# Two hand-written order lists of a fused attention and feed-forward kernel, written out anew

## The chip, the cores and the metric

The kernel runs on 1 core of one Trainium2 chip. The time is device microseconds (us). Before the change it is 468.69 us, the median of 3 runs (467.51 to 470.2). The profiled execution took 468.16 us.

## The reference

```python
def sm_attn(qq, kk, vv):
    s = scale * np.matmul(qq, kk.transpose(0, 1, 3, 2))
    s = s - np.max(s, axis=-1, keepdims=True)
    a = np.exp(s)
    a = a / (np.sum(a, axis=-1, keepdims=True) + 1e-09)
    return np.matmul(a, vv)
p_packed = sm_attn(p, k, v)                    # q, k, v: (8, 8, 576, 64), p: (8, 8, 32, 64)
out = sm_attn(q, p_packed, p_packed)
x = out.transpose(0, 2, 1, 3).reshape(4608, 512)
h = np.maximum(np.maximum(x @ w1, x @ w2), x @ w3)   # (512, 768) each
return h @ w_out                                     # (768, 512)
```

All data are float32. There are 8 batches (B) of 8 heads; a batch has 576 query rows.

## The kernel before, in words

The kernel works batch by batch. For each batch it computes the scores of the 32 packed queries with the keys (stage S), their softmax (A, Z), turns that round (X, by a write to DRAM and four reads back), multiplies it with the values (V), turns the result (K), computes the scores of the real queries (Q) and their softmax (B). The packed values are multiplied with the three weight matrices once for each of six column blocks j (stage P, `project`), and the result is multiplied with the attention weights (stage N, `layer_in`); halves and differences of the maxima (H) go through the output matrix (stage O, `layer_out`), and F adds up and stores. From batch 2 on, N is a product scheme with fewer multiplications (`layer_fast`), which needs sums of operands: T (`blend`) makes those of the attention weights, and `nine`, in P, those of the weights.

Nothing chooses the order at run time. Two strings, START (batches 0 and 1 and the conversion of the weights) and LOOP (one steady batch, run for batches 2 to 7), are lists of words, and `run` takes one word after the other. A word names a stage, the batch offset, the block and, by a last letter, an engine: v is VectorE (DVE), a is ScalarE (ACT), g is GpSimd (POOL). Each stage is a Python generator; each word carries it on to its next `yield`. So the words of N04 in LOOP are 19 steps of batch b, block 4, and `P10` is a step of the next batch, block 0. Each engine, and the DMA queue of SyncE (SP), gets its instructions in the order of the list, and works them off in that order. Where a word has the same stage and step in two lists, it issues the same instructions, but for the engine.

Small letters are loads on the SP queue: k keys, v values (two transfers each, L157 and L158), q queries, w weights at the start, m a block of the converted weights (768 KB, read back from DRAM, L171). `m03` to `m05` are blocks 3 to 5 of this batch, `m12`, `m10`, `m11` those of the next. The third word of X issues the write to DRAM (`xk<-x`, L315) and the four reads (`xt<-xk`, L319), which wait for that write.

Buffers are shared by tag. Tag "w" has six: they hold the m blocks, the scaled weights `pt` of `nine`, the sums `u` of `layer_fast` and the attention weights `e`. A tile that is asked for gets a buffer whose last tile is done, mostly the one done longest, so the order of the list also sets what each load waits for. In the list of before, `m05` gets the buffer of `u` of N00, which is free after the last join of N00 (L573 on DVE).

In `layer_fast`, three copies move sums out of PSUM (steps 7, 10 and 14, L118 on ACT, L120 on another engine):

```python
copy(u[:, 1], ps)            # step 7
join(u[:, 1], three, u[:, 1], ALU.max)
copy(u[:, 2], one)           # step 10, before product(one, (4, ...)), step 15
join(u[:, 0], two, u[:, 0], ALU.max)
copy(u[:, 3], ps)            # step 14
```

Of the kernel before, what the change touches and what calls it, by code (L numbers as in the profile page):

```python
# [47 lines left out]
B011v C10 C12 B010v N00 A10 N00 N00 A11 w20 w21 B001g B001 A10 C12 B000g A11 B011 Z10 E000a C10 A10v N00 A11a V101  # L48
C12 w22 C12 B001a q10 q11 B011v E000 C40 w52 B011g w51 Z11 C40 P01 E000 C41 V101 B001v P01 C42 k20 K1 C41 N00 C40
C40 E001a C42 N00 C41 w50 P01 C42 N01 k21 N01 C21 C20 N01 C20 C21 E010v E001 N01 C41 C42 w32 E010 P04 P04 C22 C20  # L50
K1v N01 C20 E001 w30 E011v E010 C22 N01 w31 P04 C52 Q1 N04 C21 C22 E011 H00g B11 N04 B10 B11 C52 w64 w60 C21 C22 N04
w65 C52 B10 C51 P02 E040a P02 E040 B11g B10g E011 C50 N04 N04 P02 E041a E040 N04 C51 B11 C50 C51 C50 v20 E041 N02 S2
N02 C51 B11 E041 N02 B10 C52 B11a B11 N02 C50 A20 H00a A21 B10 P05 P11 E020a v21 A20 A21 N02 B11g B10v C30 N02 P05
E020 C31 C32 C30 B10 X2 E021v w62 P05 H01g C32 N05 E021 N05 N05 B10g N05 C30 C30 E020 C31 E050a w63 C64 B11 E021 C32
P11 N05 C31 C64 B10 E050 B11a E050 N05 C32 P11 B10a B10v P12 C65 C31 E051a P12 C65 B11v X2 E051 Z21 P03 N11 N11
E110a N11 w61 N11 P03 E110 E111a H01g N11 N11 P03 N03 E030a P15 E110 H00v C62 D2g C65 H01v C61 P12 P15 P10 E051 H01v
H04g N03 C64 N03 H01a C65 N03 H02v E111 E030 Z20 N03 C62 C64 E031a N12 H04a E111 X2 P15 C60 N03 E030 N12 E031 W2v
H05a N12 C60 D5v W2v C60 W2v V201 H01g P10 P14 D5 H02a N12 E120a P10 C61 N12 N12 E121a E031 W2a C61 D1v H04v C60
E120 V201 E120 N15 H02v C63 N10 C61 N10 C62 P14 W0v N10 E121 P14 C63 C62 N14 C63 W0v C63 E100a E150a E140a E121 N14
E100 W1v N14 W2v N14 W1g E140 W2a E100 N10 N14 E140 W1g E101a W0v q21 H05v W1a E141a N10 W2v P13 K2 W1v E141 N15 q20  # L60
E101 W0a N15 N15 W1a W2g W0v W1v E151a W1g N10 H12v E150 P00 D3g E101 O0 W0a P13 F0a D3 E150 K2a H11a H03a N14 N15
W2a P13 H05v N13 k30 E130a H10v H05v D2 O0 H03v W1a N13 W0v Q2 H12a F0a E151 H05a H10a N13 O0 N13 H03v E141 E130 W1g
B20 B20 E130 B20v O0 P00 H14v W0g E131a N15 N13 N13 D0v H03g D4v O0 P20 B21 P21 O0 E151 H14a B21 F0a W2g E131 W0a
E131 H03a H12g H05v H03v H11g H10v P20a F0a H14g D0 B20 P20 F0 F0 O0 B20 P20 P20 B20a H15a O0 D1 F0 P20 O1 P20 B20
B21v B21 O1 F1a O1 H15v H15v O1 B20v H11g H13a F1a B21 B21a O0 P21a W0g H11g F1a F0 B21 H13v O0 H13v H15g B21v F0
P20a O0 F0 k31 F1v H13g B21 P21 H11a O0 B20 F0 P20v H11v H15a O1 P22 H13a F1 H15v H13g O0 F0 O1 O0 O1 O1 F0 F0 P22v
O1 P22 O1 O1 B20a B21a F1 T2g P22 F0 P21 F0 B21v P20a F1 T2g T2g F1 P20v F1 F1 O1 P22 F1 B20v D4 T2a F1 F1 T2g P22g
P21 P21g P22g F1 T2a P22a T2g P21g P21a P22g P21g O1 F1 O1 F1
"""


LOOP = """
S1 A11 N00 N00 N00a N00 N00a N00 N00a m03 N00 N00 N00a N00 A11 N00 A10 A10 N00 N00a N00 N00 N00 N00 m04 N01 N01
N01a m05 N01 N00 X1 N01a N01 N01a N01 H00g X1 N01 N01a H00a N01 N01 N01 H00g Z11 N01a N01 v10 N01 N01 N01 P03
N01 P03a P03 H01g H01g P03 P03 P03 P04 P04a P03 P04 P03g P05 P03g v11 N02 P04 N02 X1 N02a P04 N02 N02a P05a N02
N02a N02 q11 N02 P05 P05 N02a N02 N02 P03a N02 N02a k20 N02 P04a N02 H01g N02 N02 N03 N03 N03a N03 N03a P05 H01g
N03 P03g P04g N02 Z10 N03a N03 P04a N03 N03a N03 P04g q10 N03 N03 H02g P05a N03v N03 N03 N03 H01a N04 H02a N03
N04 N04a N04 N04a N04 H02v N03 H01v V101 V101 N04a H03a N04 N04 N04a N04 m12 K1 N04 N04 N04a K1v N04 N04 N04 Q1
N05 N04 N05 N04 P05g P05a N05a N05 B10 H04v N05a N05 H03g m10 N05a B10 P05v N05 B11 N05 H04a N05a N05 N05 N05
N05a H03g k21 B11 N05 N05 B10g H04g N05 N05 B11g P10 B10 P10a B10 P10 P12 P10 P10 B10v P10 N05 O0 F0a P10 O0  # L80
H05a H03v m11 B11 F0a H03a O0 H05v H05g O0 F0a B10 P11 H05v H03v O0 H05a O0 B11 H05v P11a F0a B11a P12a B11 P12
B10v F0 B10 F0 O0 P11 O0 F0a B11g O0 B11 P12 P10a P11 T1g F0a B10a B11a F0a O0 P11 T1g F0a O0 F0 B11v F0 P12 T1v
P11a P10v P10v T1a B10v O0 T1v T1a F0a O0 F0a T1g P10g P12a P12g P11g P12a P12g P11a O0 F0 F0 P11g
"""


# [780 lines left out]
```

## Time and profile before

| | |
|---|---|
| median of 3 runs | 468.69 us |
| profiled execution | 468.16 us |
| its span, first to last instruction | 466.4 us |
| PE (TensorE matmul) busy | 447.6 us, 96% |
| DVE busy | 396.7 us, 85% |
| ACT busy | 279.3 us, 60% |
| POOL busy | 262.2 us, 56% |
| mean granted TensorE clock | 0.996 of full speed |

The span is some 1.8 us shorter than the execution's time. PE is busy nearly throughout, so the few microseconds in which it is not are what an order can win or lose. Batches 0 and 1 end at about 141 us; then each steady batch takes 53 to 58 us, and the last one 50.

### The profile page before, as it was taken

The numbers are of one execution on the slowest core, as the hardware profiler recorded it, in microseconds if no ns is written. First come the engines' busy times: TensorE is split into PE (matmuls) and PEld (weight loads), VectorE is DVE, ScalarE is ACT, GpSimd is POOL, SyncE is SP. The second block draws the span as 40 slices with busy tenths as digits, with TensorE's granted clock in tenths as the row PEclk, the third lists the DMA queues.
The fourth block names the chain that finished last, engine by engine and source line by source line (L and its number), as shares of the span: only waits on it lengthen the run. The fifth ranks groups of instructions, "written<-read, shape, count | busy, mean of one in ns | idle before, by whom it ended". The sixth has DMA issues, their size and how long they took to land.

```text
span 466.4 us, 11887 instructions
## 1 busy us (share of the span) xinstructions
PE 447.6 (96%) x4592; PEld 388.5 (83%) x4592; DVE 396.7 (85%) x868; ACT 279.3 (60%) x639; POOL 262.2 (56%) x250
## 2 busy tenths in 40 slices
PE   8999999999999989999899999997999989998997
PEld 3467878998998878979799888986989878897997
DVE  2888999999987979988898989986899888987870
ACT  2687957554535737567476657754576564665652
POOL 0577775556587833856446653656337574385622
PEclk9999999999999999999999999998999999999999
DMA  8999872065248782297624784186741775235002
GB/s 305 402 381 410 281 245 81 1 199 229 84 171 282 206 341 74 92 303 237 239 85 157 275 293 178 52 264 196 265 153 66 275 208 199 69 109 197 1 2 101
DMA packets 31160, 89.89 MB, mean 193 GB/s; under 512 B 3072, under 2 KB 16384, under 8 KB 31104
## 3 DMA queue, kind: packets, MB, share of 16 engines
q1 hardware_dynamic: 31104, 89.14, 54.9%
q8 instruction: 36, 0.59, 0.5%
q14 instruction: 20, 0.16, 0.1%
HBM read 71.43 MB, written 17.69 MB: 191 GB/s over the span
## 4 chain that ended last, share of the span: by engine, by line
PE 80%; DMA 10%; DVE 7%; issue 1%; ACT 0%; POOL 0%; SPq 0%; DVEq 0%; POOLq 0%
PE mo L713 29%; PE mi L644 9%; PE mi_b L567 8%; PE mi_a L567 7%; PE pw L526 5%; DMA w<-wk 5%; DMA q<-in_qt 5%; PE mi_f L567 5%; PE mi_d L567 4%; PE idle L131 3%; PE mi_c L567 3%; PE s L367 2%; PE s L253 2%; DVE r L658 1%; DVE u L573 1%
## 5 line engine op out<-in xcount | busy, mean ns | idle before, releaser
L678 POOL TENSOR_TENSOR r<-r 128x288 f32<-128x288 f32 (+1 forms) x43 | 42.2, 982 | 38.2 <-DVE r L573 28.9
L567 PE MATMUL mi_b<-a2h,pt 128*128 128x288 f32 x216 | 47.1, 304 | 0.0
L526 PE MATMUL pw<-w,pt 64*32 64x384 f32 x768 | 38.2, 491 | 8.3 <-DMA w<-wk 7.7
L118 ACT COPY u<-mi_b 128x288 f32<-128x288 f32 x36 | 14.4, 400 | 52.9 <-PE mi_b L567 52.9
L573 DVE TENSOR_TENSOR u<-mi_d,u 128x288 f32<-128x288 f32 x72 | 32.4, 451 | 13.0 <-ACT u L118 9.0
L713 PE MATMUL mo<-ych,xh 128*128 128x288 f32 x144 | 42.6, 296 | 0.3 <-DVE r L735 0.3
L713 PE MATMUL mo<-ych,xl 128*128 128x288 f32 x144 | 42.6, 296 | 0.0
L713 PE MATMUL mo<-ycl,xh 128*128 128x288 f32 x144 | 42.1, 292 | 0.0
L567 PEld LDWEIGHTS mi_b<-a2h,pt 128*128 128x128 f32 x216 | 34.7, 190 | 8.4 <-issue 5.3
L644 PE MATMUL mi<-a2h,ph 128*128 128x288 f32 x132 | 40.4, 306 | 0.8 <-DVE r L658 0.8
L644 PE MATMUL mi<-a2l,ph 128*128 128x288 f32 x132 | 38.9, 295 | 0.6 <-DVE a2l L123 0.6
L644 PE MATMUL mi<-a2h,pl 128*128 128x288 f32 x132 | 39.0, 295 | 0.0
L481 DVE SCALAR_TENSOR_TENSOR pt<-pw,pt 128x384 fp32r<-128x384 f32 (+1 forms) x48 | 34.5, 747 | 4.4 <-ACT pt L479 4.3
L485 DVE SCALAR_TENSOR_TENSOR pf<-pw,pf 128x128 f32<-128x128 f32 (+1 forms) x108 | 35.8, 332 | 2.5
L207 POOL TENSOR_TENSOR w<-w,wi 128x512 int32<-128x512 int32 x18 | 23.7, 1327 | 23.2 <-ACT wi L192 17.3
L567 PE MATMUL mi_b<-a2l,pt 128*128 128x288 f32 x108 | 32.1, 297 | 0.0
L123 POOL TENSOR_TENSOR ps<-pf,ps 128x384 fp32r<-128x384 f32 x30 | 30.3, 1017 | 2.5 <-ACT ps L118 2.0
L567 PE MATMUL mi_a<-a2h,pt 128*128 128x288 f32 x144 | 31.0, 297 | 0.0
L479 ACT ACTIVATE pt<-pw 128x384 fp32r<-128x384 f32 (+1 forms) x48 | 29.6, 658 | 2.2 <-DVE pf L507 1.9
L567 PE MATMUL mi_f<-a2h,pt 128*128 128x288 f32 x144 | 30.3, 299 | 0.0
L644 PEld LDWEIGHTS mi<-a2h,ph 128*128 128x128 f32 x132 | 24.8, 188 | 6.5 <-issue 2.3
L401 POOL TENSOR_TENSOR e<-e,m 128x576 f32<-128x576 f32 (+1 forms) x15 | 15.9, 1070 | 24.2 <-DVE m L399 24.1
(180 smaller groups left out, 1582.8 us busy)
## 6 DMA issues: line engine op xcount, KB each, us to landing
w<-wk SPq DMA_DIRECT2D x33, 768.0 KB, 5.5
kt<-in_kp SPq DMA_DIRECT2D x16, 640.0 KB, 6.9
wi<-in_wi SPq DMA_DIRECT2D x18, 512.0 KB, 8.1
v<-in_va SPq DMA_DIRECT2D x16, 512.0 KB, 7.5
q<-in_qt SPq DMA_DIRECT2D x14, 576.0 KB, 6.4
wk<-w SPq DMA_DIRECT2D x6, 768.0 KB, 5.2
xk<-x SPq DMA_DIRECT2D x6, 576.0 KB, 7.9
wi<-in_wo SPq DMA_DIRECT2D x6, 512.0 KB, 4.4
```

The lines of the kernel that those rows point to most:

```text
L123: on(default).tensor_tensor(out=lo, in0=src, in1=hi.bitcast(F32), op=ALU.subtract)
L207: nc.gpsimd.tensor_tensor(out=dst.bitcast(I32), in0=dst.bitcast(I32), in1=up, op=ALU.add)
L401: on("g").tensor_tensor(out=e3, in0=e3, in1=m.unsqueeze(2).to_broadcast([P, nt, NP]), op=ALU.subtract)
L479: nc.scalar.activation(out=t[:, 0, r], in_=y, func=AF.Copy, scale=2.0 ** -WS)
L481: nc.vector.scalar_tensor_tensor(out=t[:, 1, r], in0=y, scalar=2.0 ** -WS, in1=t[:, 0, r].bitcast(F32), op0=ALU.mult, op1=ALU.subtract,)
L485: mix = lambda out, a, c, op: nc.vector.scalar_tensor_tensor(out=out, in0=a, scalar=2.0 ** -WS, in1=c, op0=ALU.mult, op1=op,)
L526: nc.tensor.matmul(out=ps[r][NP * n:NP * n + NP, 0:NW * P], lhsT=pt_sb[b % 2][o, NP * n:NP * n + NP], rhs=w[o, n * NW * P:(n + 1) * NW * P ...
L567: nc.tensor.matmul(out=out, lhsT=x, rhs=y, start=(start and k == 0 and n == 0), stop=(stop and k == len(terms) - 1 and n == 2), skip_group ...
L573: join = lambda out, x, y, op: nc.vector.tensor_tensor(out=out, in0=x, in1=y, op=op)
L644: nc.tensor.matmul(out=sums[b, j, hf, x][:, 0:HS], lhsT=w[:, r, x * P:(x + 1) * P], rhs=a[:, c], start=(r == 0 and n == 0), stop=(r == R - ...
L678: less = lambda out, x, y: on("g").tensor_tensor(out=out, in0=x, in1=y, op=ALU.subtract)
L713: nc.tensor.matmul(out=ps[:, 0:HS], lhsT=w[:, x, m * P:(m + 1) * P], rhs=h[:, z], start=(not chain and p == 0 and i == 0), stop=(p == NQ - ...
```

## The change

Both lists hold the same words as before in another order (START from its eighth line on, 660 words; LOOP, 285 words), and some words name another engine. No instruction is added or removed. In LOOP, what changes on each queue is this:

- PE: P04 and P05 stand behind the first two products of N02 (before: ahead of them); V101 stands behind the 15th step of N04 (before: behind the 6th), K1 after the step that follows it; Q1 stands behind the first product of N05 (before: ahead of it); P11 stands behind the sixth O0 (before: behind the fourth). All else is in the same order.
- SP before: m03, m04, m05, v10, v11, X1 (write and reads), q11, k20, q10, m12, m10, k21, m11, stores. After: m03, m04, v10, m05, X1, v11, q10, q11, m10, m12, k20, k21, m11, stores.
- Buffers of tag "w", by the order of the list: `m05` gets that of `pt` of block 0, free after step 15 of N00 (PE); `m10` that of `m05`, free after P05; `m11` that of `pt` of block 5, free after step 15 of N05.
- Engines: copies 7, 10 and 14 of N00, 14 of N01 and 10 of N04 go from ACT to DVE, 14 of N03 from DVE to ACT; K1's copy goes from DVE to ACT; five splits (of H01, H04, P10, B11 and the first of T1) go from DVE to POOL, two (P04, P05) from POOL to DVE; some smaller copies change too.

```diff
 LOOP = """
-S1 A11 N00 N00 N00a N00 N00a N00 N00a m03 N00 N00 N00a N00 A11 N00 A10 A10 N00 N00a N00 N00 N00 N00 m04 N01 N01
-N01a m05 N01 N00 X1 N01a N01 N01a N01 H00g X1 N01 N01a H00a N01 N01 N01 H00g Z11 N01a N01 v10 N01 N01 N01 P03
-N01 P03a P03 H01g H01g P03 P03 P03 P04 P04a P03 P04 P03g P05 P03g v11 N02 P04 N02 X1 N02a P04 N02 N02a P05a N02
...
-N04 N04a N04 N04a N04 H02v N03 H01v V101 V101 N04a H03a N04 N04 N04a N04 m12 K1 N04 N04 N04a K1v N04 N04 N04 Q1
-N05 N04 N05 N04 P05g P05a N05a N05 B10 H04v N05a N05 H03g m10 N05a B10 P05v N05 B11 N05 H04a N05a N05 N05 N05
...
+m03 S1 N00 N00 A11 N00a N00 m04 N00a N00 A10 v10 A11 N00v A10 N00 N00 N00v N00 m05 N00 N00 N00v N00 N00 N00 N00
+N00 N01 N01 N01a N01 N01a N01 X1 H00g H00g X1 N01a H00g N01 N01 N01a N01 N01 N01 N01v N01 N01 N01 P03 N02 N02
+P03a P04 N01 N01 P03 X1 P03 P03 P03 N02a P03 P05 N02 P04v N02a P04 N02 P05a P04 v11 N02a H01g P05 N02 H01g P04
+N02 N02a P03g q10 H01g N02 P03g q11 N02 P05 H01g m10 P04a N02 N02a N02 N02 N02 N03 N03 N03a N03 N03a N03 N02
...
+N04 N04 N04a N04 N04a N04 N04a P04a P05a N03 N04 N04 N04v N04 N04 H03a P04g k20 H02v Z10 N04 N04a N04 V101 H03g
+N04 V101 N04 K1 N04 N05 N04 K1a k21 Q1 N05 N05a N05 N05a H04v N05 P05v N05a B10 N05 B11 B10 N05 N05a N05 N05
...
```

START's lines change in the same manner, from the first H00 on: the order of the words of batches 0 and 1, of the last loads (w61 now ahead of w64, X2 ahead of w62 and w63, v20 behind them) and of the stores of the converted weights (D0 to D5), and some engines.

## Rows read from the trace of the kernel before

**Rows 1.** The page: the span, and section 1 (busy time, share, instructions).
```profile
span 466.4 us, 11887 instructions
PE 447.6 (96%) x4592; PEld 388.5 (83%) x4592; DVE 396.7 (85%) x868; ACT 279.3 (60%) x639; POOL 262.2 (56%) x250
```

**Rows 2.** Busy time by stretch: its length, then each engine, PEclk, DMA.
```profile
80.00:100.00 20.00, 19.21 (x154) 18.15 (x153) 19.48 (x39) 12.37 (x24) 9.29 (x8) 1.00 0.24 80
...
140.80:195.30 54.50, 52.89 (x574) 46.99 (x581) 48.11 (x107) 34.14 (x83) 32.55 (x33) 1.00 0.60 205
195.30:250.40 55.10, 52.74 (x572) 46.87 (x576) 49.24 (x109) 33.97 (x83) 30.46 (x31) 1.00 0.58 197
250.40:303.60 53.20, 52.81 (x570) 46.94 (x570) 48.87 (x109) 34.08 (x83) 30.63 (x31) 1.00 0.59 204
303.60:361.10 57.50, 54.24 (x573) 48.35 (x576) 49.03 (x109) 34.08 (x83) 30.45 (x31) 0.97 0.56 189
361.10:416.00 54.90, 52.67 (x567) 46.94 (x567) 48.78 (x109) 33.96 (x83) 30.46 (x31) 1.00 0.52 173
```

**Rows 3.** Who PE waited for: us in total, times, longest.
```profile
PE pw L526 <- DMA w<-wk: 7.7, 4, 3.2
PE s L367 <- DMA q<-in_qt: 2.7, 3, 1.2
```

**Rows 4.** The chain that ended last, batch 3: start us, us, what.
```profile
195.29 1.13 PE s L253 x32
...
200.19 0.41 PE mi_a L567 x3
...
202.43 5.41 DMA w<-wk
...
216.20 8.66 DMA q<-in_qt
```

**Rows 5.** The same chain in batches 4 to 7.
```profile
250.42 1.13 PE s L253 x32
...
260.52 2.14 PE pw L526 x48
262.66 0.99 PE mi_b L567 x6
...
310.78 7.55 DMA w<-wk
...
319.25 1.74 PE mi_b L567 x6
...
368.26 6.53 DMA w<-wk
...
422.15 5.71 DMA w<-wk
```

**Rows 6.** The SP queue in batch 3: start us, us, what.
```profile
213.23 1.97 SPq L319 DMA_DIRECT2D xt<-xk  x4
```

**Rows 7.** Time to landing: the w issued at 198.0, the v at 205.1.
```profile
DMA to landing us min/median/max: 6.8/6.8/6.8
...
DMA to landing us min/median/max: 6.5/6.5/6.5
```

**Rows 8.** DVE, then weight loads of PE, after V101 in batch 3.
```profile
221.12 0.48 DVE L349 TENSOR_SCALAR pp<-av,r 128x64 f32<-128x64 f32 x2 [0.56 <-PE av L339]
...
221.75 0.14 PEld L354 LDWEIGHTS av<-ident,pp 128*128 128x128 f32 x1
```

**Rows 9.** DVE from 141 to 416 us by form: busy us, mean ns.
```profile
L123 DVE TENSOR_TENSOR a2l<-e,a2h 128x576 fp32r<-128x576 f32 x15 | 18.2, 1236 | 0.0
...
L266 DVE TENSOR_REDUCE mx<-s 128x1 f32<-128x576 f32 x10 | 7.5, 746 | 0.8 <-PE s L253 0.8
...
L123 DVE TENSOR_TENSOR ybl<-r,ybh 128x576 fp32r<-128x576 f32 x5 | 3.8, 751 | 0.0
...
L120 DVE COPY u<-mi_f 128x288 f32<-128x288 f32 x5 | 2.3, 456 | 1.0 <-PE mi_f L567 1.0
```

More of the change, by code (lines that the diff above doesn't have):

```diff
@@ L50 @@
 C40 E001a C42 N00 C41 w50 P01 C42 N01 k21 N01 C21 C20 N01 C20 C21 E010v E001 N01 C41 C42 w32 E010 P04 P04 C22 C20
[L51 to L68, printed above, removed]
+K1v N01 C20 E001 w30 E011v E010 C22 N01 w31 P04 C52 Q1 N04 C21 C22 E011 E011 H01a N04 H00g C21 N04 B10 H00a B10 C22
@@ new lines @@
+E040a B11 E040 P02 B11 C51 H00v C51 v21 N04 C51 C52 B10g B11v w61 P02 C50 E041a N04 N04 C50 C50 C52 C50 P02 B11 C32
+w64 C32 B10 B11 S2 E040 w60 N02 w65 E041 A20 A21 C30 A20 N02 B11a C51 B10 N02 C32 H01v H01g C52 E020a A21 E020 P05
+P11 X2 C31 N02 P05 P05 B10a E021a C30 E020 C32 N02 B10 H01g N05 C30 C31 X2 B11 N05 C61 E041 C64 B10g C31 B11v E021
+P12 C60 N05 C31 E050a P11 C30 B10 E050 B11 N05 N02 C61 P11 N05 B10a E051a C64 X2 w62 B11a C65 E021 B10g N05 E051
+B11v C65 P03 w63 H02v P03 N11 N11 E051 C65 P12 E050 H01a N11 v20 P03 C64 N11 E110a H01v P15 E110 N03 C60 N11 E111a
@@ new lines @@
+P12 C65 C60 N11 C61 E030a C63 E111 N03 P15 N03 N12 C63 H02a C64 N03 Z20 C62 E111 N12 N03 V201 C61 E030 E110 Z21 P10
+E030 C60 W2v N03 E031a H04v C62 D5v W0v W0g P15 E031 W2v N12 W2g H11a E120a N12 H02v W0v C62 C63 W2a E031 E120 P10
+N12 N12 H05a E121a V201 P10 P14 E120 C62 C63 W1g N15 W2v P14 H03a E121 E150a P14 N10 E121 N15 W0a W1g E150 E100a
+H04a K2 P13 N14 W1v H12v W0v H05g E140a N15 N14 N10 N14 W2a D4g D4 N10 W0a N10 N15 N10 N14 E150 E100 E140 D5 H04v
+W1a E101a N14 H03v q20 E100 E151a K2v N10 W2v q21 H05g E141a W1v W2g N14 E140 O0 E141 O0 W0g E101 W1a P13 E101 W1v
@@ new lines @@
+E141 P13 W0g O0 O0 H14v N13 D2v H03v Q2 H05v F0a F0a H03v H05a O0 D0v D1v N13 H05v B21 F0a O0 H10g H12a H14a B20 k31
+F0a F0 H11g E130a B21 E130 H03a B20 H12g D1 F0 N15 W2a W0a W2g N13 W0v N13 E151 B21v W1g N13 N15 N13 B20v H03v H10a
+H14v E131a E130 E131 H10g B21 P21 P22 E151 B20 H11g P20 P21a B20 E131 O1 O1 O1 O1 P20a H15a B21 P20 H11v O0 W1a W1v
+B21a D0 B21 F1a F1a H15v H13a B21v H15g F1a P22a D3v B20a H15v O0 O0 O0 P21 P20 F1a O0 H13g O0 P20 P20 F0 B20 P20
+H15a O0 H13g B20g B21 F0 F0 F0 H13g F0 H13a D3 H11a B20 F0 P21 O0 F0 P00 F0 H15v O1 H13v H11v F0 O1 B20a k30 T2v F0
@@ L69 @@
+O1 T2g B21a P21 P20a P00 P21a B20g F1 T2g O1 F1 P20g P22 F1 D2 F1 B21v T2a O1 O1 F1 F1 P22 P22 F1 F1 P21g O1 P21g F1
+O1 F1 T2g O1 P21g P22g O1 P20a T2a T2g P22g F1 P22a F1 P22v P20v
 """
 LOOP = """
-S1 A11 N00 N00 N00a N00 N00a N00 N00a m03 N00 N00 N00a N00 A11 N00 A10 A10 N00 N00a N00 N00 N00 N00 m04 N01 N01
-N01a m05 N01 N00 X1 N01a N01 N01a N01 H00g X1 N01 N01a H00a N01 N01 N01 H00g Z11 N01a N01 v10 N01 N01 N01 P03
-N01 P03a P03 H01g H01g P03 P03 P03 P04 P04a P03 P04 P03g P05 P03g v11 N02 P04 N02 X1 N02a P04 N02 N02a P05a N02
@@ L76 @@
-N02a N02 q11 N02 P05 P05 N02a N02 N02 P03a N02 N02a k20 N02 P04a N02 H01g N02 N02 N03 N03 N03a N03 N03a P05 H01g
-N03 P03g P04g N02 Z10 N03a N03 P04a N03 N03a N03 P04g q10 N03 N03 H02g P05a N03v N03 N03 N03 H01a N04 H02a N03
-N04 N04a N04 N04a N04 H02v N03 H01v V101 V101 N04a H03a N04 N04 N04a N04 m12 K1 N04 N04 N04a K1v N04 N04 N04 Q1
-N05 N04 N05 N04 P05g P05a N05a N05 B10 H04v N05a N05 H03g m10 N05a B10 P05v N05 B11 N05 H04a N05a N05 N05 N05
-N05a H03g k21 B11 N05 N05 B10g H04g N05 N05 B11g P10 B10 P10a B10 P10 P12 P10 P10 B10v P10 N05 O0 F0a P10 O0
@@ L81 @@
-H05a H03v m11 B11 F0a H03a O0 H05v H05g O0 F0a B10 P11 H05v H03v O0 H05a O0 B11 H05v P11a F0a B11a P12a B11 P12
-B10v F0 B10 F0 O0 P11 O0 F0a B11g O0 B11 P12 P10a P11 T1g F0a B10a B11a F0a O0 P11 T1g F0a O0 F0 B11v F0 P12 T1v
-P11a P10v P10v T1a B10v O0 T1v T1a F0a O0 F0a T1g P10g P12a P12g P11g P12a P12g P11a O0 F0 F0 P11g
+m03 S1 N00 N00 A11 N00a N00 m04 N00a N00 A10 v10 A11 N00v A10 N00 N00 N00v N00 m05 N00 N00 N00v N00 N00 N00 N00
+N00 N01 N01 N01a N01 N01a N01 X1 H00g H00g X1 N01a H00g N01 N01 N01a N01 N01 N01 N01v N01 N01 N01 P03 N02 N02
@@ new lines @@
+P03a P04 N01 N01 P03 X1 P03 P03 P03 N02a P03 P05 N02 P04v N02a P04 N02 P05a P04 v11 N02a H01g P05 N02 H01g P04
+N02 N02a P03g q10 H01g N02 P03g q11 N02 P05 H01g m10 P04a N02 N02a N02 N02 N02 N03 N03 N03a N03 N03a N03 N02
+P03g N02 N03a N03 P04v H01a N03 N03a Z11 P05 P03g H02g N03 N03 N03 N03a N03 N03 H02a N03 P05a N03 m12 P05v H01g
+N04 N04 N04a N04 N04a N04 N04a P04a P05a N03 N04 N04 N04v N04 N04 H03a P04g k20 H02v Z10 N04 N04a N04 V101 H03g
+N04 V101 N04 K1 N04 N05 N04 K1a k21 Q1 N05 N05a N05 N05a H04v N05 P05v N05a B10 N05 B11 B10 N05 N05a N05 N05
@@ L84 @@
+H04g H04g H03g m11 N05 N05a N05 B10g B11 N05 N05 P10 P12 O0 N05 P10a N05 O0 O0 P10 P10 P10 P12a P10 P10 O0 B10
+B10 H05a F0a H05v O0 F0a H03v H05g B11g B11 O0 B10v P11 H05v B10 B11 F0a P10a H03a H03v F0a H05a H05v B11a B11
+B10v P10g B10 P12 F0 B11g F0 B11 O0 F0a O0 P12 O0 P10a B10a T1g T1v T1v F0a B10v P11a O0 F0a F0a P11 T1a F0 F0
+O0 P12 B11a B11g P11 T1g O0 F0a P11 O0 F0a P11a P12a T1a F0 T1g O0 P12g P12a F0 P11g P10v P12g P11g P11g
 """
```

## The prediction

> **What bounds the kernel now.** I read the page first: PE is busy for 447.6 of 466.4 us, more than any other engine [rows 1], and the work of no engine changes in amount, only in place. So the change can only win the time in which PE stands still, or add to it. The table of stretches then shows where that is. A steady batch holds 52.8 us of PE work (52.89, 52.74, 52.81 and 52.67 in the four batches at full clock), but the five batches from 140.8 to 416 take 54.5, 55.1, 53.2, 57.5 and 54.9 us, together 275.2 [rows 2]. 275.2 less 5 x 52.8 is 11.2 us. The list of PE's waits names the cause: 7.7 us in four waits of `pw` for a block of weights, 2.7 us in three waits of Q1 for queries, and nothing else in the steady batches comes to 1.5 us [rows 3].
>
> The chain of waits shows how each comes about. In batch 3, the third block (m05) is issued at 202.43, when its buffer comes free behind three DVE joins that follow the product at 200.19 to 200.60; it lands at 207.84 [rows 4]. In batch 4 the three `pw` groups run unhindered, so P05 is due at 260.52 + 2/3 x 2.14 = 261.95, which is 11.5 us after S1 [rows 5]. In batch 3 that is 206.8, so PE waited 1.05 us. In the same way batch 5 (S1 at 303.6) waited until 318.33 instead of 315.1, 3.2 us, and batch 6 until 374.79 instead of 372.6, 2.2 us [rows 2, 5]; 7.7 less these leaves 1.25 for the last batch. The last query block in batch 3 is issued at 216.20 and lands at 224.86 [rows 4]; it stood in the SP queue behind the reads of X1, which began at 213.23 [rows 6].
>
> Behind the longest stop the mean granted clock of the batch is 0.97 [rows 2]: the first `mi_b` group takes 1.74 us where another takes 0.99 [rows 5]. The engine had stood still for 3.2 us before; the shorter stops, of 1 to 2.2 us, have no such row. These matmuls ran at the lower of the two levels (1.2 GHz, against 2.4). The row shows 0.75 us lost on the first six; PE's busy time in the batch, 54.24, is 1.5 above the mean of the others, 52.8 [rows 2], and I take that as the loss. So loads cost 11.2 + 1.25 = 12.5 us in all: 7.7 + 2.7 + 1.5 = 11.9, and 0.6 in small change.
>
> **The change part by part.**
>
> *m05 and P05.* The issue moves from 202.43 to 200.6 or so, 1.8 us, since the new buffer is free with PE's step 15 and not with the last DVE join [rows 4]. But two transfers of v10 now stand ahead of it. Their price: the last of two such pairs was issued at 205.1 and took 6.5 us, so it landed at 211.6 [rows 7], 3.8 us after the block at 207.84 [rows 4]: 1.9 us a pair. So the block lands when it did. The use moves: the first two products of N02, 9 matmuls, are put ahead of P04, some 0.8 + 0.4 us without the 0.2 for the change from narrow matmuls that is paid anyway [rows 4, 5]. Each wait shrinks by 1.2: batch 3 from 1.05 to 0, batch 5 from 3.2 to 2.0, batch 6 from 2.2 to 1.0. The last batch has no v10, so its block lands earlier and it waits 0. Left: 3.0 us. Bounds: 0, if the issue 1.8 us earlier counts as well; 9.8, if the pair comes on top without that gain (first rival). A stop of 2.0 us is among those that left the clock alone, so the 1.5 us go.
>
> The Trainium skill, page "DMA: Bandwidth & Descriptors", section "Anatomy of one DMA", puts a transfer at 2.0 us plus its bytes at 436 GB/s, measured for transfers issued by GpSimd. By it m03, m04, v10 and m05, 2.95 MB, would land 8.8 us after the first issue, no wait were left, and the sum would be 457.2. The trace does not bear it out here: m04, issued at 198.0, took 6.8 us [rows 7], so 1.57 MB landed at 204.8, about 7.6 us after the first issue, where the rule gives 5.6.
>
> *Queries and Q1.* The write of X1 no longer has v11 in front of it, so it lands a pair earlier, 1.9 us, and the reads begin near 211.3 instead of 213.23 [rows 6]. v11 comes next, then both query blocks without a key block between them; the bytes ahead of the last one are about the same (a v pair for k20), so it lands near 223. Q1 was due about 1.2 us before 224.86, stands one six-matmul product (0.8) later, and moves up by the 1.05 that P05 no longer waits: some 223.5. Wait 0 instead of 2.7. Bounds: 0 and 2.7.
>
> *v11 behind the reads.* It is issued near 213 and, at 6.5 us [rows 7], lands near 219.5. V101 ends at 221.05 today and takes 1.4; its place is 2.0 us later and the batch 1.05 earlier: due at 220.6. Cost 0, and nothing less; if v11 is late by more than 1 us, a microsecond a batch, at most 5.
>
> *K1.* Today two products (0.8 us) lie between V101 and K1, which turns what DVE makes of V101. DVE is done with it at 221.60, 0.55 after V101, and K1's weights load at 221.75 [rows 8]. Now one product of 0.4 us lies between. PE then waits 0.7 - 0.4 = 0.3 us, in five batches 1.5. Bounds: 0 and 2. The copy behind K1 goes to ACT; K1 and a copy of 0.3 fit under the product of 0.8 that now precedes Q1, at a cost of 0 to 1.5 if ACT is late. I take 0.
>
> *m10, m12, m11, keys.* m10 and m12 are issued earlier and used as before; m11 waits for N05's step 15 instead of P10, and P11 stands two products of O0 (2.4 us) later. All gain room; k20 and k21 are due a batch half later. 0, with no gain either, as PE never waited for them [rows 3].
>
> *Engines.* By the mean durations of like rows, DVE loses about 0.9 us a batch of 49, ACT 3.3 of 34, and POOL gains 4.3 on 30.5 [rows 2]. None reaches 52.8. So 0; what it costs if DVE is late at one place is the second rival.
>
> *START.* From 40 us on DVE is as full as PE (19.48 and 19.21 of 20 us in the stretch shown [rows 2]). The new engines take some 3 us from DVE, and PE's words are in quite another order. PE idles under 1 us in each such stretch, so there is little to win: 0, from -2 to +2.5. The upper end: V201 stands three PE words of some 0.8 us earlier, and waits that long if its loads, whose order changed too, come as before.
>
> *Sum.* The profiled execution took 468.16 us (its span of 466.4 and 1.8 around it), 0.5 under the median of the runs. 468.16 - 12.5 + 3.0 (P05) + 1.5 (K1) = **460.2 us**.
>
> **Rivals.** *The v pair is paid in full (no change).* If blocks queue strictly and the queue was full anyway, m05 lands 1.9 us later than today. Then P05 waits 1.75, 3.9 and 2.9 us in batches 3, 5 and 6 and 0.6 in the two others with v10, 9.8 in all, and the clock still falls once: 468.16 - 12.5 + 9.8 + 1.5 + 1.5 = 468.5. For it: m04, m05 and the v transfers landed in the order of issue, about 3 and 1.9 us apart [rows 4, 7]. Against it: m05 was issued 5.2 us after m03, and the queue had little to move before it began.
>
> *DVE is late in N00 (slower).* Copies 7, 10 and 14 of N00 go to DVE, behind two reductions of 746 ns with a small step each [rows 9]. From S1's end, at 196.4, 1.8 for these, 0.46 for copy 7, 0.45 for a join and 0.46 for copy 10 [rows 9] make 199.6 to 199.7; step 15, which needs copy 10, starts at 200.19 [rows 4]. So 0.5 us is spare. If DVE comes to S1 later than that, PE waits for the excess, in all six batches: at 2 us 12 us, 472.2. It decides against the change from 8 / 6 = 1.3 us on. For it: the split of `a2l` on DVE takes 1236 ns on average where a like split of `ybl` takes 751 [rows 9], so DVE is held up near a batch's start, and POOL gets more to do. Against it: that split is one that leaves DVE for POOL, and DVE's sum falls.
>
> The Trainium skill, page "SBUF — State Buffer", section "SBUF: two separate sides", says that DVE and GpSimd share one port pair, held for a whole instruction, and that a DVE operation with two SBUF inputs takes part in this. By that rule the three copies, which read PSUM, are not held up at all, and this rival would be worth nothing; the row of the split agrees with it, for the copies no run shows it here.
>
> *The opening loses, or the loads are all covered.* With START at +2.5 and Q1 not wholly covered, some 465; with no wait left at P05 and K1, 455.7.
>
> **How the numbers follow.** Forecast, 457 to 464: 0.55. All covered, 455.7: 0.10. Opening loses, 465: 0.08. The pair paid in full, 468.5: 0.15. DVE late, 472: 0.12. I hold half a percent, 2.3 us about the median of 468.7, for what a measurement can tell from no change. Faster: 0.55 + 0.10 + 0.08 = 0.73; same: 0.15; slower: 0.12. The range reaches from 455.0 to 468.6 and leaves out the slower case and a little below; beside it, the likeliest case's own range is 457 to 464.
>
> **What would show it.** In PE's waits, `pw` for `wk` at about 3 us instead of 7.7, in two waits, and Q1 for `q` gone; a granted clock of 1.00 in every stretch; steady batches of 53 to 55 us. In the chain, m05 issued 5.3 us after S1 instead of 7.1. A gap of 0.3 us between V101 and K1, ended by DVE's `pp`. Wrong would be waits of `pw` that stay above 6 us, a gap in N00 that ends with a DVE copy, or a first 141 us that grew by more than 2.5.

## The result, and the profile after

The changed kernel took 463.46 us (median of 4 runs, 463.06 to 463.78), the kernel before beside it 469.44: a ratio of 0.9871, 95% interval 0.9826 to 0.9917. The profiled execution took 463.06 us against 468.16. A second series (12 runs, given below) put the same kernel at 465.23 and a ratio of 0.9941 (0.9910 to 0.9971). So the change makes the kernel faster by something between 0.6 and 1.3% (the two intervals reach from 0.3 to 1.7%); the forecast of 460.2 had the direction and lies below both. Ratios, here and below, leave out runs that lie more than 1.5% above the fastest of the same kernel.

The page: the span, and the engines' busy time.

```profile
span 461.3 us, 11953 instructions
PE 451.7 (98%) x4592; PEld 387.7 (84%) x4592; DVE 395.4 (86%) x885; ACT 262.1 (57%) x600; POOL 283.0 (61%) x272
```

The five steady batches by stretch (columns as in [rows 2]).

```profile
139.50:194.00 54.50, 54.00 (x567) 47.02 (x566) 50.22 (x112) 30.16 (x75) 34.03 (x33) 1.00 0.58 204
194.00:248.30 54.30, 53.79 (x574) 47.09 (x579) 49.25 (x111) 31.04 (x78) 34.59 (x35) 1.00 0.57 200
248.30:302.50 54.20, 53.70 (x572) 46.99 (x573) 49.25 (x111) 30.97 (x78) 34.52 (x35) 1.00 0.57 200
302.50:356.70 54.20, 53.69 (x567) 46.99 (x566) 49.25 (x111) 30.95 (x78) 34.49 (x35) 1.00 0.57 200
356.70:410.90 54.20, 53.71 (x567) 47.18 (x567) 49.26 (x111) 30.98 (x78) 34.54 (x35) 1.00 0.50 176
```

Before, a batch took whatever the loads allowed, 53.2 to 57.5 us [rows 2]. Now all five are alike, 54.2 to 54.5, at full clock, and 271.4 together instead of 275.2. But none is near the 52.8 that the forecast took for a batch without load waits. The list of PE's waits from 141 us on says why:

```profile
PE mi_a L567 <- ACT mi_b L118: 1.8, 6, 0.4
PE mi_d L567 <- DVE u L573: 1.3, 6, 0.2
```

Both load waits of [rows 3] are gone, 10.4 us. In their place stand two waits that occur once in every batch, and PE's busy time in a batch is some 0.9 us higher than before: a matmul that starts late is in part booked as a long one, as the chain shows. This is the chain in batch 3 (start, us, what), at N01, at N02 and at K1, in three pieces. In it `mi_a` to `mi_f` are the PSUM banks of a product, `u` holds the sums copied out of them, `r` the maxima of a block; `pt` and `pf` are the scaled weights that `nine` makes.

```profile
199.86 0.47 DVE u L573
200.33 0.02 issue
200.35 0.77 DVE r L573
...
201.20 0.41 ACT u L118
201.61 0.02 issue
201.63 0.39 ACT mi_b L118
202.02 0.04 issue
202.07 0.67 PE mi_a L567 x3
...
209.44 0.96 DVE pt L481
210.39 0.21 DVE pf L485
210.60 0.02 issue
210.62 0.43 DVE pf L485
...
211.29 0.46 DVE u L573
211.75 0.04 issue
211.79 0.66 PE mi_d L567 x3
```

```profile
222.26 0.59 PE mi_d L567 x3
222.85 0.03 issue
222.88 0.33 PE av L354
```

First piece: the first copy of N01 (`u`, ACT) starts only when DVE has finished N00's last join (`r`, to 201.12), because it writes into the buffer of N00's `u`. That is the buffer that `m05` had before the change. `m05` now has the one that comes free earlier, and the wait that it used to bear has passed to N01's copy, then to the second copy (`mi_b`), then to PE: three `mi_a` matmuls take 0.67 instead of 0.40. Together with the gap before it that is 0.54 us a batch. Second piece: DVE makes P04's scaled sums (`pt`, `pf`) ahead of N02's join `u`, and N02's last product waits; 0.6 us a batch by the steps of N02. Third: K1, foreseen.

`m05` itself, with its time to landing, and P05's place on PE (the 32 narrow matmuls are P04 and then P05, 16 each, so P05 starts near 207.5):

```profile
L171 SPq DMA_DIRECT2D w<-wk x1: 320/320/320, 199.5 to 199.5; - x1
...
DMA to landing us min/median/max: 7.5/7.5/7.5
```

```profile
206.84 1.52 PE L526 MATMUL pw<-w,pt 64*32 64x384 f32 x32
```

It is issued 5.5 us after S1 (194.0), lands 12.9 us after it, and is used 13.5 us after it.

### The profile page after: what moved, and what is told of

It is laid out like the page before. It is cut to its first block, busy times and chain, and to the rows that moved or that the text cites. A ratio compares the mean times of both kernels' runs of the same rounds, so it can differ in the third digit from the quotient of the medians.

```text
span 461.3 us, 11953 instructions
## 1 busy us (share of the span) xinstructions
PE 451.7 (98%) x4592; PEld 387.7 (84%) x4592; DVE 395.4 (86%) x885; ACT 262.1 (57%) x600; POOL 283.0 (61%) x272
## 3 DMA queue, kind: packets, MB, share of 16 engines
q1 hardware_dynamic: 31104, 89.14, 54.2%
## 4 chain that ended last, share of the span: by engine, by line
PE 84%; DVE 7%; DMA 3%; ACT 2%; issue 2%; SPq 1%; POOL 0%; DVEq 0%; ACTq 0%; POOLq 0%
PE mo L713 30%; PE mi L644 12%; PE mi_a L567 8%; PE mi_b L567 7%; PE mi_d L567 6%; PE pw L526 6%; PE mi_f L567 5%; PE idle L131 3%; PE mi_c L567 2%; PE s L253 2%; PE av L339 2%; PE s L367 2%; DMA xk<-x 2%; DMA xt<-xk 1%; DVE pt L481 1%
## 5 line engine op out<-in xcount | busy, mean ns | idle before, releaser
L678 POOL TENSOR_TENSOR r<-r 128x288 f32<-128x288 f32 (+1 forms) x45 | 43.7, 972 | 36.6 <-DVE r L573 28.9
L123 POOL TENSOR_TENSOR ps<-pf,ps 128x384 fp32r<-128x384 f32 x24 | 24.2, 1018 | 13.3 <-ACT ps L118 13.3
L567 PE MATMUL mi_a<-a2h,pt 128*128 128x288 f32 x144 | 32.3, 305 | 0.0
L123 POOL TENSOR_TENSOR ybl<-r,ybh 128x576 fp32r<-128x576 f32 x15 | 26.1, 1743 | 9.4 <-DVE w L177 3.7
```

What stands on the lines that cost most here:

```text
L123: on(default).tensor_tensor(out=lo, in0=src, in1=hi.bitcast(F32), op=ALU.subtract)
L567: nc.tensor.matmul(out=out, lhsT=x, rhs=y, start=(start and k == 0 and n == 0), stop=(stop and k == len(terms) - 1 and n == 2), skip_group ...
L678: less = lambda out, x, y: on("g").tensor_tensor(out=out, in0=x, in1=y, op=ALU.subtract)
```

## The experiments

In the edited kernels the lines are numbered one higher, since the lists are wrapped anew. The excerpts of the lists are cut at both ends. The kernel before spreads widely (463.3 to 474.8 in 29 runs of one series, median 468.1), so lengths of batches in the traces say more than ratios.

**loop_only**: the new LOOP, the old START.

```diff
 LOOP = """
-S1 A11 N00 N00 N00a N00 N00a N00 N00a m03 N00 N00 N00a
...
+m03 S1 N00 N00 A11 N00a N00 m04 N00a N00 A10 v10 A11
...
```

> The new LOOP with the old START. Theory A (the loop's load waits are gone, but three new small waits of some 1.4 us a batch stand in their place): about 4 us less than before, 464.5, steady batches of 54.2 us, no load wait of PE. Theory B (the opening carries what was gained): within 1.5 us of before.

464.67 us, ratio 0.9936 (0.9914 to 0.9959). Batches of 54.2 us, no load wait. Theory A holds. All 12 runs lie between 464.41 and 464.94: the spread of 11 us that the loads gave the kernel before is gone.

**start_only**: the new START, the old LOOP.

```diff
 START = """
...
-w65 C52 B10 C51 P02 E040a P02 E040 B11g B10g E011 C50
...
+E040a B11 E040 P02 B11 C51 H00v C51 v21 N04 C51 C52 B10g
...
```

> The new START with the old LOOP. Theory A: about 1.3 us less than before, 467; the waits of pw and Q1 for loads are as before, 8 to 11 us. Theory B: 463 to 464.

465.63 us, ratio 0.9969 (0.9926 to 1.0011). In time it lies between the two theories and is not told from no change. By its waits it is theory A, just under its 8 us: `pw` waits 7.5 us and Q1 0.3 for loads, so the load waits belong to the old LOOP. Its S1 of batch 2 is at 139.4, 1.4 before [rows 2]; the last section shows why the opening has no one length.

**before_v11_late**: one word of the old LOOP moved.

```diff
-P03g v11 N02 P04 N02 X1 N02a
+P03g N02 P04 N02 X1 v11 N02a
```

> The kernel before with one word moved: the second v pair is issued behind the reads of X1, not right behind the first pair. Theory A (transfers issued behind m05 take a share of the queue's rate from it): m05 lands up to 2 us earlier in batches 5 and 6, the waits of pw fall from 7.7 to 3 to 4.5 us, Q1's wait falls to under 1, time about 463 to 465. Theory B (the queue works in the order of issue): m05 lands as before and pw waits 7 to 8 us; only Q1's 2.7 us can go, time 466 or above.

Theory A fell, and theory B held only in part: `m05` lands as before, but `pw` waits longer than its 7 to 8 us. 473.28 us, ratio 1.0127 (1.0066 to 1.0188).

```profile
PE pw L527 <- DMA w<-wk: 9.3, 4, 2.9
PE s L368 <- DMA q<-in_qt: 1.6, 1, 1.6
PE s L368 <- DVE r L574: 1.5, 1, 1.5
PE av L340 <- DMA v<-in_va: 0.5, 1, 0.5
```

`m05`, issued 7.2 us after S1 as before, landed after 11.4, 14.4, 11.4, 13.6 and 14.4 us, as scattered as before (11.3, 12.6, 11.4, 14.8 and 13.7); taking the v pair away from behind it did not make it land earlier. X1's write is issued a microsecond earlier here, close behind `m05`; whether that took its share was not tried. Two batches ran at a mean clock of 0.97 instead of one, and V101 now waits for its values. Moving a load later on SP is no gain by itself.

**before_pe_late**: two words of the old LOOP moved.

```diff
-P03 P03 P03 P04 P04a P03 P04 P03g P05 P03g v11 N02 P04 N02 X1
+P03 P03 P03 N02 N02 P04 P04a P03 P04 P03g P05 P03g v11 P04 X1
```

> The kernel before with the first two products of N02 put ahead of P04, nothing else. Theory A: P05 is due 1.4 us later, the waits of pw fall from 7.7 to about 3, the slow clock of batch 5 goes, time 462 to 464. Theory B (the loads set the pace, so a later use is only waited for elsewhere): less than 1.5 us gained.

463.4 us, ratio 0.9906 (0.9870 to 0.9941), and `pw` waits 4.1 us in five waits of 1.0 at most. Theory A.

```profile
PE pw L527 <- DMA w<-wk: 4.1, 5, 1.0
PE s L368 <- DMA q<-in_qt: 1.9, 2, 1.0
```

One move of two words does as much as the whole new LOOP: it removes half of the waits of `pw` and the slow clock, and adds no wait that comes back in every batch.

**after_again**: the changed kernel, as the measure for the three that follow.

> The changed kernel once more, unaltered, as the measure for the three kernels beside it: 463 to 464, every execution within 1 us.

465.23 us: three runs at 463.0 to 463.3 and nine at 464.7 to 466.5. The expectation missed the second group. In its profile P05 waits for `m05` once, 0.5 us in batch 5. N02's wait is missing in that batch, and the batch takes 54.24 us like its neighbours.

**after_join**: the join of N02 one DVE step earlier.

```diff
-H01g P04 N02 N02a P03g
+H01g N02 P04 N02a P03g
```

> The changed kernel with N02's first join put ahead of P04's second step on DVE (two words swapped). Theory A (this join comes late because the scaled sums of P04 stand ahead of it on DVE, and N02's last product waits for it): the wait of mi_d for DVE's u goes, 0.5 us a batch in six batches, 3 us less than the changed kernel. Theory B (the longer steps there are the change from narrow to wide matmuls, not a wait): no gain, under 0.5 us.

465.57 us, batches of 54.27: nothing gained, yet the wait named by theory A went. Another of the same size took its place, `mi_b` of N03 for an ACT copy:

```profile
PE mi_b L568 <- ACT u L119: 1.9, 6, 0.3
```

**after_join2**: besides, N02's last copy ahead of P04's on ACT.

```diff
-m10 P04a N02 N02a N02
+m10 N02 N02a P04a N02
```

> The changed kernel with N02's first join ahead of P04's second step on DVE, as tried before, and besides N02's last copy ahead of P04's copy on ACT. Theory A (two queues were late by the same half microsecond, DVE for mi_d of N02 and ACT for the bank that mi_b of N03 needs): both waits go, 0.4 to 0.5 us a batch, a batch of 53.8 us, 2.5 to 3 us less than the changed kernel. Theory B (a third wait takes the place): batches stay above 54.1 us.

465.63 us, batches of 54.23. Theory B: now N03's second product waits for a third.

```profile
PE mi_a L568 <- ACT mi_b L119: 1.8, 6, 0.4
PE mi_a L568 <- DVE u L574: 1.7, 6, 0.5
```

So the half microsecond at N02 is not a misplaced word: DVE and ACT are behind by that much, and PE meets it at whichever step comes next. That P03 to P05 standing so close is the reason is my reading of the chain; no run spread them apart with all else as it is.

**after_v101**: V101 one product earlier.

```diff
-N04 N04a N04 V101 H03g N04 V101 N04 K1 N04
+N04 N04a V101 N04 H03g V101 N04 N04 K1 N04
```

> The changed kernel with V101 put one product earlier, so that two products lie between V101 and K1 as in the kernel before. Theory A (K1 waits 0.2 to 0.3 us for DVE in each of five batches): 1.0 to 1.5 us less than the changed kernel, K1 without a wait. Theory B (the time there is the change of matmul shape): under 0.4 us.

462.43 us, 2.8 under the changed kernel beside it. Its batches take 53.99 against 54.23, which makes 1.2 of that. The rest I put down to the opening: four of the six runs lie at 461.9 to 462.6 and two near 464, but only one of them has a trace. Theory A: behind two products K1 (`av`) starts at once.

```profile
222.07 0.59 PE mi_a L568 x3
222.66 0.39 PE mi_d L568 x3
223.06 0.11 PE av L355
```

**after_m05_back**: `m05` behind N01's first copy.

```diff
-N00v N00 m05 N00 N00 N00v N00 N00 N00 N00 N00 N01 N01 N01a N01 N01a
+N00v N00 N00 N00 N00v N00 N00 N00 N00 N00 N01 N01 N01a N01 m05 N01a
```

> The changed kernel with m05 put behind N01's first copy, so that m05 and that copy exchange buffers, as in the kernel before. Theory A (the copy waits for N00's last join, because it got the buffer that m05 had): the wait of mi_a for ACT in N01 goes, 0.5 us a batch, 3.2 in all; m05 is issued 7.1 us after S1 instead of 5.5 and lands at 13 to 14.5, P05 is due at 13.0, so pw waits 0 to 1.5 us in each batch: 461.5 to 465.5, and a wider spread of the executions. Theory B (ACT is late for its own work): the wait in N01 stays at 0.3 to 0.4 us a batch.

462.37 us, 2.9 under the changed kernel beside it. Batches of 53.70, 0.53 less. Theory A: the wait in N01 goes with the buffer. `m05`, issued at 7.1, landed after 11.6 to 14.3 us, and one of six waits was left, in batch 5:

```profile
PE pw L527 <- DMA w<-wk: 1.2, 1, 1.2
PE mi_d L568 <- DVE u L574: 1.1, 5, 0.2
```

In that batch N02's wait is missing again, and the batch takes 54.32, 0.6 longer than its neighbours for a wait of 1.2. So what DVE and ACT lack at N02 is 0.6 us, and a wait ahead of it is paid only as far as it exceeds that.

**after_v10_behind**: `v10` issued behind `m05`.

```diff
-N00 A10 v10 A11 N00v A10 N00 N00 N00v N00 m05 N00
+N00 A10 A11 N00v A10 N00 N00 N00v N00 m05 v10 N00
```

> The changed kernel with the first v pair issued behind m05 instead of ahead of it. Theory A (the pair ahead costs m05 1.9 us, as the prediction had it): m05 lands 1 to 2 us earlier after S1 than the 11.4 to 14.2 of the changed kernel, and no wait of pw is left; the time moves by less than 0.7 us. Theory B (transfers that run together share the rate, so it matters little which is issued first): m05 lands within 0.7 us of where it did.

465.19 us, batches of 54.23. `m05`, issued at 5.5, landed after 10.3, 10.6, 11.0 and 12.1 us in batches 3 to 6, 11.0 on average, where the two executions of the changed kernel have 12.9, 11.5, 12.6, 11.8 and 12.8, 11.5, 14.2, 11.4, together 12.3. The pair costs some 1.3 us: theory A, at two thirds of the 1.9 that I had priced. The sign is clear, since three of the four landings are earlier than every one of the eight; the size rests on four landings where the eight spread over 3 us.

**best_a**: all of it (after_join2, after_v101, after_m05_back), and P05 behind N02's third and fourth product. **best_b**: the same with `v10` behind `m05`.

```diff
-P03 P05 N02 P04v N02a P04 N02 P05a
+P03 N02 P04v N02a P04 N02 P05 P05a
```

> The changed kernel with all that the runs point to: m05 and N01's first copy exchange buffers, V101 one product earlier, the two moves of N02, and P05 two products later (behind N02's third and fourth), so that m05 has 0.8 us more. Theory A (the small waits are independent and add up): 54.2 - 0.54 - 0.25 - 0.45 = 53.0 us a batch, 456 to 458 in all. Theory B (they are one slack that is passed on): 53.5 us a batch or more, 459 or above.

> The same with the first v pair issued behind m05. Theory A (the pair ahead of m05 costs it 1.9 us): m05 lands earlier, the waits of pw that are left in best_a go, up to 1.5 us less than it. Theory B (shared rate): the same as best_a within 0.7 us.

463.76 and 463.46 us, batches of 53.87 in both. The time fits theory B for the first, but the run does not decide between the two, since it holds a fifth move, that of P05. One wait is left, and that move made it.

```profile
PE mi_c L568 <- DVE pf L486: 2.7, 6, 0.5
```

With P05 gone from its place, PE comes to N02's third product 0.7 us earlier than DVE has emptied the PSUM bank that `mi_c` needs (`pf` reads it). Theory B for the second: whether `v10` stands ahead of `m05` makes no difference when `m05` is issued at 7.1 (landing at 12.6 on average in both). The two single edits, after_m05_back and after_v101, have the lowest medians, by 1 us, which is less than the two lengths of the opening differ by. By length of batch after_m05_back is first (53.70), the two combinations come next (53.87), then after_v101 (53.99). The two single edits together, without the rest, were not run.

## Why the prediction was right, and where its terms were off

*What bounds the kernel.* Right: 12.5 us hung on loads, and in the profiled execution all of it went, the slow clock of batch 5 too. The sum was 468.16 - 12.5 + 4.5; the execution gives 468.16 - 5.1, which is 2.9 more. By the terms below, -12.5 + 0 + 1.2 + 6.8 - 1.3 makes -5.8; 0.7 stays unassigned. That the number came within 2.9 us is in part luck: the 6.8 us that the sum lacked were offset by 3.0 at P05, 0.3 at K1 and 1.3 in the opening. One reading behind the 12.5 did not hold: that a stop of 2.0 us leaves the clock alone. In start_only a wait of 2.0 us in batch 5 was followed by a granted clock of 0.74 (317 to 322 us), and in before_v11_late one of 2.0 in batch 5 by 0.75 (323 to 328), while one of 2.8 in its batch 6 left that batch at 1.00. The length of the stop alone does not tell; here it cost nothing, since no stop was left.

*m05 and P05: 3.0 forecast, 0 measured* (a wait of 0.5 in after_again, which lengthened nothing). The issue, 5.5 us after S1, and the landing in batch 3, 12.9 against 12.55 before, came as forecast. The use moved further than I had it: P05 is due at 13.5, not 12.7. The two products take 1.4 with the change from narrow matmuls, not 1.2, and N01's new wait holds PE back by 0.5 more: part of the cover is itself a loss. The forecast took the landings of batches 5 and 6 (7.55 and 6.53 us [rows 5]) for fixed. They scatter, but not by chance alone: in the seven traces with `m05` issued at 7.1 or 7.2, batch 5 has it land after 13.5 to 14.7 us and batch 4 after 11.4 to 12.4, once 14.1. What sets a batch apart stays open.

*Queries.* No wait, as forecast, and with far more room: in batch 3 the last block lands 4 us before Q1, since X1's write, issued at 202.84, took 5.5 us and the reads began at 208.38, not 211.3.

*K1: 0.3 a batch forecast, 0.24 measured* by after_v101, 1.2 in five. Right. The copy behind it cost nothing, as taken.

*Small waits that the sum lacked: 0 forecast, 1.14 us a batch measured, 6.8 in six* (0.54 by after_m05_back; 0.6 by the steps of N02 and by batch 5 of after_m05_back). This is the step that failed. In "Engines" I compared sums by engine with 52.8 and found room; nothing followed each new place in its own queue. N01's copy (0.54) could have been read off the text that I had written myself: if `m05` takes the buffer that N01's `u` used to take, then N01's `u` takes the other. I priced the exchange for `m05` alone. N02 (0.6) comes, by the chain, of P03, P04 and P05 moving together with N02's start, so that the `pt` and `pf` of these blocks meet N02's joins on DVE. DVE's busy time rose by 0.4 us a batch where I had it fall by 0.9; ACT's fell by 3.1 and POOL's rose by 4.0, as forecast.

*START: 0 forecast, -1.3 in the profiled execution.* Over the runs, 0 was the better number (464.67 with the old START, 463.46 and 465.23 with the new). S1 of batch 2 starts at 140.6 to 141.3 in four traces with the old START, and in ten with the new one either at 139.4 to 140.4 (five) or at 141.0 to 142.6 (five). The last section has what sets the two apart.

*Rivals.* The v pair paid in full: no, 1.3 us and covered. DVE late in N00: no; in batches 3 to 6 no step of N00 is late, and the three copies take 0.46 each. That side was right to weigh, but the loss came in N01 and N02.

*The rule of the Trainium skill on a transfer* (page "DMA: Bandwidth & Descriptors", section "Anatomy of one DMA", 2.0 us plus bytes at 436 GB/s) would have had `m05` land 8.8 us after the first issue; in batch 3 it took 11.9 (195.07 to 206.96), so the trace disagrees and the wait went for other reasons.

## What to carry to other kernels

Buffers that rotate by order of release are a ring: a load that is given an earlier buffer hands the later one to somebody, and the price has to be followed to that tile. Where one load lands up to 3 us later in one batch than in another, moving its use by 1.4 us (two words) bought as much as rewriting the issue order. A list can be made insensitive to its loads, and that shows first in the spread of the runs; the half microseconds that pay for it recur in every batch and show only in part as idle time of the busy engine.

## What the runs showed of the hardware

The opening has two lengths. These are DVE and POOL in the same stretch, in the changed kernel's first execution and then in after_again (start, us, engine, line, operation), the first two lines DVE's, the others POOL's:

```profile
100.61 1.28 DVE L177 TENSOR_TENSOR w<-w 128x512 f32<-128x512 f32 x2
101.81 1.05 DVE L123 TENSOR_TENSOR ycl<-r,ych 128x864 fp32r<-128x864 f32 x1
...
100.83 3.33 POOL L123 TENSOR_TENSOR ybl<-r,ybh 128x576 fp32r<-128x576 f32 x1 [3.38 <-PE mo L713]
104.12 1.43 POOL L123 TENSOR_TENSOR yal<-r,yah 128x576 fp32r<-128x576 f32 x1
```

```profile
100.72 2.52 DVE L177 TENSOR_TENSOR w<-w 128x512 f32<-128x512 f32 x2
103.16 2.28 DVE L123 TENSOR_TENSOR ycl<-r,ych 128x864 fp32r<-128x864 f32 x1
...
100.94 1.75 POOL L123 TENSOR_TENSOR ybl<-r,ybh 128x576 fp32r<-128x576 f32 x1 [3.38 <-PE mo L713]
102.65 1.88 POOL L123 TENSOR_TENSOR yal<-r,yah 128x576 fp32r<-128x576 f32 x1
```

Same program, same order. In the one, DVE's two subtractions and the split take 2.3 us and POOL's split is held to 3.33; in the other POOL's goes through in 1.75, DVE's second subtraction lasts until 0.55 after POOL's end, and its split waits in the same way. DVE then comes out 2.5 us later, and S1 of batch 2 is 2.0 us later on average (141.8 against 139.8 in the five traces each). All ten traces with the new START agree: POOL's split takes 3.33 in the five with the early S1 and 1.75 in the five with the late one. The traces with the old START show no such pair. The Trainium skill, page "SBUF — State Buffer", section "SBUF: two separate sides", has the rule: DVE operations with two SBUF inputs and GpSimd share a port pair, and whichever starts first holds it for its whole instruction. The trace agrees: 3.33 against 1.75 us for one POOL instruction, and none of the copies out of PSUM was stretched. That the outcome can differ from run to run, and that it splits the runs of one kernel into two groups 2 us apart, I had not expected. No kernel was run that takes the pair apart, so that the pair causes the two lengths rests on the ten traces.
